# A row test of a DFT matrix, cut into pieces that alternate between two buffers, in an FNet and GLU kernel

## The chip, the core and the metric

The kernel runs on one core of a Trainium2 chip. The core has a matrix engine (TensorE, "PE" in the profile, its weight loads "PEld"), a vector engine (VectorE, DVE), an engine for activation functions (ScalarE, ACT), GpSimd (POOL) and SyncE (SP), which here issues nearly all DMAs. Each engine works through its own queue in order; semaphores tie the queues together. Sixteen DMA engines move the data. The metric is the device time of one execution in microseconds.

## The reference

Two kinds of layers are applied in turn, twice each, to x of 2048 rows and 640 columns. The first is a Fourier layer, given as dense matrices; the second a gated linear unit. The matrices and weights are inputs:

```python
def _A_ref(x, dft_seq_re, dft_seq_im, dft_hid_re, dft_hid_im):
    a = jnp.einsum("bsd,ed->bse", x, dft_hid_re)
    b = jnp.einsum("bsd,ed->bse", x, dft_hid_im)
    y = jnp.einsum("ts,bse->bte", dft_seq_re, a) - jnp.einsum("ts,bse->bte", dft_seq_im, b)
    return y

def _B_ref(x, w_gate, w_up, w_down):
    g = jnp.einsum("bsd,df->bsf", x, w_gate)
    u = jnp.einsum("bsd,df->bsf", x, w_up)
    h = _sigmoid(g) * u
    return jnp.einsum("bsf,fd->bsd", h, w_down)

x = x + _A_ref(_layernorm(x, axis=-1), A_dft_seq_re, A_dft_seq_im, A_dft_hid_re, A_dft_hid_im)
x = x + _B_ref(_layernorm(x, axis=-1), B_w_gate, B_w_up, B_w_down)
...
```

The inner width of the gated unit is 1728. After the two lines shown, both are applied once more.

## The kernel before

**Tiling.** The rows of x live in SBUF for the whole run, 16 tiles of 128 rows. One wide buffer (`big`) holds everything else: it is counted in units of 128 float32 columns, a planner (`Slots`) hands out ranges of units, and behind the planner's range lie two fixed buffers of 8 units, the *rooms* 0 and 1 (`room(k)`, with k taken modulo 2). All products are made of float16 parts: a matrix is split into a high part (on ACT, L236) and a low part (on DVE, L238), and three of the four cross products are summed in PSUM.

**Stages.** Each of the two layers has a Fourier stage and a gated stage. The Fourier stage folds rows and columns that a DFT matrix repeats with equal or opposite sign, so that a quarter of the work is left. Its results come back in four *quads* of row tiles: `combine` (L910), `join_hidden` (L917) and `add_hidden` (L930) add each quad's results to the rows of x, all on DVE. The gated stage goes over four blocks of 512 rows. In each block, gate and up products run over 14 column tiles j of the weights (13 of 128 and a tail), and then the down product (L1232) runs over four row tiles in two halves each. Block 0 uses `gate_up` (L1039), one step for each j. Blocks 1 to 3 use `seven` (L1085 with PSUM copies L1089 on ACT), one for each two j, a form with seven products in place of eight; it reads weights that `load_s` fetches with three DMAs (L1010, L1012, L1013: 320, 512 and 192 KB), and a transposed x that `pair_transpose` (L504) makes with DMA transposes before the block begins.

**Tests.** The folded way is right only if the DFT matrices have the symmetries of a DFT. So the kernel also reads the matrices whole and tests them: differences (or sums) of entries that should cancel are squared and summed on ACT (`square_sum`, L1264, one new column of `dsum` for each), and largest values are taken on DVE. At the end `test_all` compares the sums with a tolerance and sets a flag; if it is set, a plain version (`general`) runs after all. The matrix `ct` over rows is tested in both layers, in 42 pieces each, through the two rooms. The matrix `wh` over columns (real and imaginary, 640 by 640) is tested in the second layer alone, from the third down stage to the end of the last block's gate and up stage. `load_hidden(j)` loads 64 rows of both parts into room 0 and the 64 mirrored rows, in reverse order, into room 1 (L1339, two DMAs of 320 KB). `test_hidden(j)` takes the largest value (L1342), subtracts or adds the mirrored rows for each part (L1345) and the mirrored columns (L1346), and puts three squares on a list; `square_rest` makes them. Five such tests, each over both rooms, and one of row 0 cover the matrix.

**Order.** The instructions of every engine are laid out by a hand-made plan. The products are a list of *steps*; `at(u, f, ...)` puts other work at a place u in steps, and before each step (or within a `seven`, which spans two, in four places) the work due by then is issued to the queues. `block[b]` is the step at which the gate and up stage of block b begins; a block is 22 steps, 14 for gate and up and 8 for down. So a load at `block[2] + 15.5` is issued within the down stage of block 2. A queue is not reordered afterwards: an instruction that waits holds up all that stand behind it on its engine. SP's DMAs use eight semaphores in turn, so that a DMA is also behind the one issued eight before it.

Of the kernel before, what the change touches and what calls it, by code (L numbers as in the profile page):

```python
# [30 lines left out]
EC = EH + 1  # L31
# [147 lines left out]
@with_exitstack  # L179
def kernel(ctx: ExitStack, tc: tile.TileContext, x, ct, wh, wg, wu, wc, wd, out):  # L180
    nc = tc.nc
    pool = ctx.enter_context(tc.tile_pool(name="sb", bufs=1))
    psum = ctx.enter_context(tc.tile_pool(name="ps", bufs=1, space=bass.MemoryType.PSUM))
    dram = ctx.enter_context(tc.tile_pool(name="dr", bufs=1, space=bass.MemoryType.DRAM))

    big = pool.tile([P, (UNITS + 2 * CK) * UNIT], F32, name="big")
    acc = [psum.tile([P, 512], F32, name=f"acc{i}") for i in range(6)]
    flag = pool.tile([P, 1], I32, name="flag")
    with tc.manual_schedule():
        folded(ctx, tc, pool, dram, big, acc, flag, x, ct, wh, wg, wu, wc, wd, out)  # L190
    bad = nc.values_load(flag[0:1, 0:1], min_val=0, max_val=1,
                         skip_runtime_bounds_check_because="it is the result of a comparison")
    with tc.If(bad != 0):
        with tc.manual_schedule():
            general(tc, big, [acc[2 * i : 2 * i + 2] for i in range(4)], x, ct, wh, wg, wu, wc, wd, out)


def folded(ctx, tc, pool, dram, big, acc, flag, x, ct, wh, wg, wu, wc, wd, out):
    nc = tc.nc
# [60 lines left out]
    def at(u, f, *a):  # L260
        jobs[max(0, int(u // 1))].append((u, f, a))
# [993 lines left out]
    def new_sum():  # L1255
        n_sum[0] += 1
        return dsum[:, n_sum[0] - 1 : n_sum[0]]

    def new_max():
        n_max[0] += 1  # L1260
        return cmax[:, n_max[0] - 1 : n_max[0]]

    def square_sum(v, p=0):
        nc.scalar.activation(v, v, AF.Square, accum_out=new_sum()[p : p + v.shape[0]])  # L1264

    rest = []

    def square_rest():
        square_sum(*rest.pop(0))

    def room(k, n=CK):
        u = UNITS + CK * (k % 2)
        return big[:, u * UNIT : (u + n) * UNIT]
# [8 lines left out]
    def test_rows(r, k):  # L1282
        v = room(k)
        a, b, c, d = (v[:, 2 * P * g : 2 * P * (g + 1)] for g in range(4))
        same, other = (OP.subtract, OP.add) if r == 0 else (OP.add, OP.subtract)
        nc.vector.tensor_tensor(b, a, b, op=same)  # L1286
        nc.vector.tensor_tensor(d, c, d, op=same)
        for odd in range(2):
            nc.vector.tensor_tensor(c[:, odd::2], a[:, odd::2], c[:, odd::2], op=other if odd else same)  # L1289
        rest.append((v[:, 2 * P :], 0))  # L1290

    def load_cols(r, i, k):

# [5 lines left out]
    def test_cols(r, i, k):  # L1299
        v = room(k)[: P if i < NB else 1]  # L1300
        a, d, c, b = (v[:, 256 * g : 256 * (g + 1)] for g in range(4))
        same, other = (OP.subtract, OP.add) if r == 0 else (OP.add, OP.subtract)
        nc.vector.tensor_reduce(new_max()[: a.shape[0]], a, axis=AX.X, op=OP.max, apply_absolute_value=True)
        nc.vector.tensor_tensor(b, b, a[:, ::-1], op=same)
        nc.vector.tensor_tensor(d, d, c[:, ::-1], op=same)
        nc.vector.tensor_tensor(c, c, a[:, ::-1], op=other if i in (2, 3) else same)
        rest.append((v[:, 256:], 0))

    def load_edges(r):

# [7 lines left out]
    def test_edges(r):  # L1318
        v = held["ce", r].f32
        nc.vector.tensor_reduce(new_max(), v[:, :40], axis=AX.X, op=OP.max, apply_absolute_value=True)  # L1320
        nc.vector.tensor_reduce(new_max()[0:1], v[0:1, 40:42], axis=AX.X, op=OP.max, apply_absolute_value=True)
        if r == 0:
            for a, b in ((0, 16), (32, 36)):
                for odd in range(2):
                    d = v[:, b + odd : 2 * b - a : 2]
                    nc.vector.tensor_tensor(d, v[:, a + odd : b : 2], d, op=OP.add if odd else OP.subtract)
            nc.vector.tensor_tensor(v[0:1, 41:42], v[0:1, 40:41], v[0:1, 41:42], op=OP.subtract)
            square_sum(v[:, 16:32])
            square_sum(v[:, 36:40])
            square_sum(v[0:1, 41:42])  # L1330
        else:
            square_sum(v[:, :40])
            square_sum(v[0:1, 40:42])
        drop("ce", r)

    def load_hidden(j):

        for k, (row, step) in enumerate(((1 + 64 * j, D), (D - 1 - 64 * j, -D))):
            nc.sync.dma_start(room(k)[:, :D], bass.AP(wh.tensor, row * D, [[D * D, 2], [step, 64], [1, D]]))  # L1339

    def test_hidden(j):
        nc.vector.tensor_reduce(new_max(), room(0)[:, :D], axis=AX.X, op=OP.max, apply_absolute_value=True)  # L1342
        for r, op in enumerate((OP.subtract, OP.add)):
            a, b = (room(k)[64 * r : 64 * r + 64, :D] for k in range(2))
            nc.vector.tensor_tensor(b, a, b, op=op)  # L1345
            nc.vector.tensor_tensor(a[:, 1:EH], a[:, 1:EH], a[:, D - 1 : EH : -1], op=op)  # L1346
            rest.append((a[:, :EC] if r else a[:, 1:EH], 64 * r))
        rest.append((room(1)[:, :D], 0))

    def load_hidden_first():  # L1350

        for r in range(2):
            nc.sync.dma_start(room(r)[0:1, :D], wh[r, 0:1, :])

    def test_hidden_first():
        a, b = (room(r)[0:1, :D] for r in range(2))
        nc.vector.tensor_reduce(new_max()[0:1], a, axis=AX.X, op=OP.max, apply_absolute_value=True)
        nc.vector.tensor_tensor(a[:, 1:EH], a[:, 1:EH], a[:, D - 1 : EH : -1], op=OP.subtract)
        rest.append((a[:, 1:EH], 0))
        rest.append((b, 0))  # L1360

    def test_all():

# [95 lines left out]
    for layer in range(2):  # L1459
# [10 lines left out]
        block = []  # L1470
# [23 lines left out]
        if first:  # L1494
            for b in range(NB):
# [12 lines left out]
                else:  # L1508
                    for k in range(2):
                        v = d0 + 4 * k  # L1510
# [37 lines left out]
        for q in range(1, NB):  # L1548
            for n, (f, *a) in enumerate(((combine, 0), (combine, 1), (join_hidden, 0), (add_hidden, 0), (join_hidden, 1),
                                         (add_hidden, 1))):  # L1550
                at(block[0] + 1.6 + (0.8 * n if q == 1 else 6 * q - 7 + n), f, q, *a)
        for b in range(1, NB):
            for i in range(2):
                u = block[b] - 8 + 1.2 * i
# [35 lines left out]
        if first:  # L1590
            for j in range(NF):
                if 3 <= j < NF:
                    u = block[0] + j - 1.5
                else:
                    u = block[1] - 8 + 1.5 * j
# [21 lines left out]
        at(u0, test_edges, layer)  # L1617
        if not first:
            tests = [(load_hidden, test_hidden, (j,), 3) for j in range(EH // 64)]
            tests.append((load_hidden_first, test_hidden_first, (), 2))  # L1620
            for q, (load, test, key, n) in enumerate(tests):
                u = block[2] + 15.5 + 3 * q
                at(u, load, *key)
                at(u + 2, test, *key)
                for k in range(n):
                    at(u + 2.2 + 0.25 * k, square_rest)
            at(block[3] + 16, test_all)

    for u, step in enumerate(steps):
        if step is None:  # L1630
# [4 lines left out]
                      key=lambda j: j[0])  # L1635
# [163 lines left out]
```

## Time and profile before

| What | us |
|---|---|
| three runs | 1215.63, 1217.84 (median), 1218.98 |
| the profiled execution, its own time | 1217.2 |
| its span in the profile | 1215.3 |
| first product of the first layer's block 0 (gate and up) to the last block's end in that layer | 96.89 to 625 |
| second layer's last gate and up stage | 1046.44 to 1164.25 |
| its down stage | 1164.25 to 1208.8 |

| Engine | busy us | share of the span |
|---|---|---|
| PE | 1144.1 | 94% |
| PEld | 864.6 | 71% |
| DVE | 737.7 | 61% |
| ACT | 500.7 | 41% |
| POOL | 169.1 | 14% |

How to read it: times are from the start of the span. A row of the timeline has its start, its length, engine, line, operation, what is written and read, how many, and in brackets how long the engine had been idle before it and what ended that. "big" is the wide buffer, "acc" a PSUM bank, "in_wh" the matrix over columns in HBM, "kept_w" and "kept_s" the split weights that the kernel wrote to HBM in the first layer. PEclk is the share of TensorE's clock that was granted. In the DMA rows the first is the busy share of the 16 engines in tenths and the second the rate, each in 40 equal slices of the stretch asked for. A share of a queue is the time of its packets over the time of 16 engines.

### The profile page before, as it was taken

To read this page: it belongs to the slowest core of one execution; us is meant where nothing else is said; L and a number is where in the kernel's file an instruction comes from. 1 tells how busy PE (TensorE), PEld (TensorE's weight loads), DVE (VectorE), ACT (ScalarE), POOL (GpSimd) and SP (SyncE) were. 2 spreads that over 40 slices of the span, in tenths; PEclk is the share of its full clock that TensorE was granted. 3 is DMA by queue.
4 is the path that set the end of the run, shared out by engine and by line. 5 is a ranking of instruction groups with operands and counts; after the bars stand their busy time and mean duration, and the time that the engine had idled before them with its cause. 6 is when DMAs were issued, how large, how long until landed. Compare 5 with 4: busy or idle time off the path is not lost.

```text
span 1215.3 us, 22619 instructions
## 1 busy us (share of the span) xinstructions
PE 1144.1 (94%) x8784; PEld 864.6 (71%) x8784; DVE 737.7 (61%) x1590; ACT 500.7 (41%) x1066; POOL 169.1 (14%) x361
## 2 busy tenths in 40 slices
PE   5699989999999999999999999999999999578997
PEld 2367435788878887888766645788878887457875
DVE  7694899657747675766335768556854675224430
ACT  5665444255525552565115214145533552034410
POOL 3423555210002010100011001000100010000000
PEclk9799999999999999999999999999999999879899
DMA  9352887868596959688025425879498847545301
GB/s 276 112 161 88 278 292 265 209 228 214 154 223 189 265 179 227 209 226 232 1 66 177 143 67 162 222 207 279 134 244 245 265 148 83 148 137 150 113 13 36
DMA packets 219711, 214.75 MB, mean 177 GB/s; under 512 B 67886, under 2 KB 175303, under 8 KB 219594
## 3 DMA queue, kind: packets, MB, share of 16 engines
q1 hardware_dynamic: 218954, 210.59, 59.7%
q0 software_dynamic: 640, 2.62, 0.6%
q8 instruction: 71, 1.16, 0.4%
q14 instruction: 46, 0.38, 0.1%
HBM read 169.39 MB, written 30.40 MB: 164 GB/s over the span
## 4 chain that ended last, share of the span: by engine, by line
PE 76%; DVE 6%; DMA 6%; issue 4%; ACT 3%; SPq 2%; POOL 2%; ACTq 0%; POOLq 0%; DVEq 0%
PE acc L1085 34%; PE acc L1232 25%; PE acc L1039 11%; DMA big<-in_wh 4%; PE acc L1168 2%; PE acc L845 2%; PE acc L763 2%; DVE big L238 1%; SPq L504 1%; DMA big<-kept_w 1%; ACT big L236 1%; DVE big L1064 0%; DVE big L498 0%; DVE big L1345 0%; POOL quad L397 0%
## 5 line engine op out<-in xcount | busy, mean ns | idle before, releaser
L1085 PE MATMUL acc<-big 128*128 128x256 f16 x4212 | 471.1, 275 | 28.7 <-ACT big L1089 23.4
L1085 PEld LDWEIGHTS <-big 128*128 128x128 f16 x4212 | 415.7, 99 | 81.5 <-issue 24.0
L1232 PE MATMUL acc<-big 128*128 128x320 f16 x2624 | 357.9, 299 | 0.6 <-DVE big L1219 0.6
L1232 PEld LDWEIGHTS <-big 128*128 128x128 f16 x2624 | 256.7, 98 | 100.5 <-ACT big L1218 0.9
L1089 ACT ACTIVATE big<-acc 128x256 f32<-128x256 f32 x312 | 117.1, 383 | 201.3 <-PE acc L1085 197.8
L1039 PE MATMUL acc<-big 128*128 128x512 f16 (+1 forms) x990 | 179.0, 342 | 8.0 <-DVE big L238 5.2
L1039 PEld LDWEIGHTS <-big 128*128 128x128 f16 x990 | 96.5, 98 | 89.7 <-DVE big L238 8.2
L1264 ACT ACTIVATE big<-big 128x768 f32<-128x768 f32 (+8 forms) x106 | 80.9, 763 | 164.1 <-DVE big L1289 95.0
L1153 DVE TENSOR_TENSOR big<-big 128x512 f16<-128x512 f32 x78 | 53.8, 690 | 123.4 <-ACT big L1152 123.4
L1247 DVE SCALAR_TENSOR_TENSOR big<-acc,big 128x320 f32<-128x320 f32 x64 | 28.3, 485 | 75.4 <-PE acc L1232 75.3
L1131 ACT ACTIVATE big<-big 128x512 f32<-128x512 f32 x78 | 47.8, 629 | 33.7 <-DVE big L1122 33.3
L238 DVE SCALAR_TENSOR_TENSOR big<-big 128x640 f16<-128x640 f32 (+6 forms) x81 | 59.1, 769 | 3.3 <-ACT big L236 3.2
L1286 DVE TENSOR_TENSOR big<-big 128x256 f32<-128x256 f32 x64 | 26.7, 417 | 52.6 <-DMA big<-in_ct 52.3
L1141 DVE SCALAR_TENSOR_TENSOR big<-acc,big 128x256 f32<-128x256 f32 x78 | 32.7, 419 | 39.4 <-PE acc L1085 32.8
L236 ACT ACTIVATE big<-big 128x640 f16<-128x640 f32 (+6 forms) x81 | 49.9, 668 | 15.6 <-DMA big<-big 4.6
L763 PE MATMUL acc<-big 128*128 128x256 f16 (+5 forms) x288 | 42.9, 309 | 12.4 <-ACT big L649 10.0
L1122 DVE TENSOR_TENSOR big<-big,acc 128x512 f32<-128x512 f32 x78 | 53.2, 682 | 2.2 <-PE acc L1085 2.0
L1152 ACT ACTIVATE big<-big 128x512 f16<-128x512 f32 x78 | 48.9, 627 | 7.1 <-DVE big L1143 5.8
L763 PEld LDWEIGHTS <-big 128*128 128x128 f16 (+1 forms) x288 | 31.1, 114 | 25.0 <-ACT big L649 12.9
L845 PE MATMUL acc<-big 128*128 128x321 f16 (+3 forms) x324 | 48.7, 301 | 0.2 <-ACT big L892 0.2
L845 PEld LDWEIGHTS <-big 128*128 128x128 f16 (+3 forms) x324 | 28.6, 96 | 19.3 <-issue 7.8
L1053 ACT ACTIVATE big<-acc 128x512 f32<-128x512 f32 x26 | 15.5, 596 | 64.1 <-DVE big L1064 34.4
(166 smaller groups left out, 990.0 us busy)
## 6 DMA issues: line engine op xcount, KB each, us to landing
big<-kept_w SPq DMA_DIRECT2D x125, 320.0 KB
big<-kept_s SPq DMA_DIRECT2D x75, 512.0 KB
big<-in_ct SPq DMA_DIRECT2D x256, 128.0 KB
big<-kept_w SPq DMA_DIRECT2D x78, 192.0 KB
kept_w<-big SPq DMA_DIRECT2D x41, 320.0 KB
big<-in_ct SPq DMA_DIRECT2D x32, 256.0 KB
kept_s<-big SPq DMA_DIRECT2D x13, 512.0 KB
big<-in_wg SPq DMA_DIRECT2D x16, 320.0 KB
```

The lines of the kernel that those rows point to most:

```text
L236: nc.scalar.activation(dh, src, AF.Copy, scale=s)
L238: nc.vector.scalar_tensor_tensor(dl, src, s, dh, op0=OP.mult, op1=OP.subtract)
L763: nc.tensor.matmul(o, xv[:, 384 * xp + c0 : 384 * xp + c0 + n], moving(r, cps[cp]), start=(i % 2 == 0 and r == 0 and xp == HI and cp == HI ...
L845: nc.tensor.matmul(ps[:m, :EC], z[:, at : at + m], w[:, 384 * wp : 384 * wp + EC], start=(d == 0 and zp == HI and wp == HI), stop=(d == ND ...
L1039: nc.tensor.matmul(ps, w[wp][:, d * P : (d + 1) * P], xt[:, xp, :], start=(d == 0 and wp == HI and xp == HI), stop=(d == ND - 1 and wp == LO))
L1085: nc.tensor.matmul(ps, wt, xt, start=start and n == 0, stop=n == len(todo) - 1, skip_group_check=not start)
L1089: nc.scalar.activation(dst, ps, AF.Copy)
L1122: nc.vector.tensor_tensor(v, v, other, op=OP.add)
L1152: nc.scalar.activation(s.parts[HI], v, AF.Copy)
L1153: nc.vector.tensor_tensor(s.parts[LO], v, s.parts[HI], op=OP.subtract)
L1232: nc.tensor.matmul(held["pd", e][0][:, :EH], held["ht", j].parts[hp][:, i * P : (i + 1) * P], held["w", 2, j].parts[wp][:, e * EH : (e + 1 ...
L1264: nc.scalar.activation(v, v, AF.Square, accum_out=new_sum()[p : p + v.shape[0]])
```

## The change

The test of `wh` is cut in another way. Symmetry over rows and symmetry over columns are now tested apart, each with its own reading of the matrix. For rows (`load_hidden_rows`, `test_hidden_rows`), each part is tested in four pieces of 80 rows and their 80 mirrored rows, eight pieces in all. A piece fits in one room: the 640 columns are five blocks of 128, a block's 80 rows stand on 20 partitions, four rows on each, so that 100 partitions are used, the rows in one half of the room and the mirrored ones in the other. Pieces alternate between the rooms. A piece needs two DMAs, one DVE operation over 512 columns and one square. For columns (`load_hidden_cols`, `test_hidden_cols`), each part's 321 first rows are read in three pieces of 128, 128 and 65 rows by 640 columns, each in one room, with a largest value, one subtraction or addition and one square each (one more square for a part of row 0). Loads, tests and squares have new places: a row piece every 1.7 steps with its test 2.8 steps after the load and its square 0.42 steps later, then a column piece every 0.9 steps with its test 1.4 steps after.

`square_sum` no longer takes a first partition; that renames lines only. And the additions of the quads in block 0 are laid out anew, in both layers: the third quad's six operations one step earlier, the last quad's six two steps later, so that all six of the last quad come after the gate and up stage, within the first down steps.

```diff
-    def square_sum(v, p=0):
-        nc.scalar.activation(v, v, AF.Square, accum_out=new_sum()[p : p + v.shape[0]])
+    def square_sum(v):
+        p = v.shape[0]
+        nc.scalar.activation(v, v, AF.Square, accum_out=new_sum()[:p])
...
-    def load_hidden(j):
-
-        for k, (row, step) in enumerate(((1 + 64 * j, D), (D - 1 - 64 * j, -D))):
-            nc.sync.dma_start(room(k)[:, :D], bass.AP(wh.tensor, row * D, [[D * D, 2], [step, 64], [1, D]]))
-
-    def test_hidden(j):
-        nc.vector.tensor_reduce(new_max(), room(0)[:, :D], axis=AX.X, op=OP.max, apply_absolute_value=True)
-        for r, op in enumerate((OP.subtract, OP.add)):
-            a, b = (room(k)[64 * r : 64 * r + 64, :D] for k in range(2))
-            nc.vector.tensor_tensor(b, a, b, op=op)
-            nc.vector.tensor_tensor(a[:, 1:EH], a[:, 1:EH], a[:, D - 1 : EH : -1], op=op)
-            rest.append((a[:, :EC] if r else a[:, 1:EH], 64 * r))
-        rest.append((room(1)[:, :D], 0))
...
+    def load_hidden_rows(r, k):
+
+        v = room(k)[: 20 * ND].rearrange("p (g n c) -> p g n c", g=2, c=P)
+        for g, (row, d) in enumerate(((1 + 80 * k, 1), (D - 1 - 80 * k, -1))):
+            nc.sync.dma_start(v[:, g], bass.AP(wh.tensor, (r * D + row) * D, [[P, ND], [d * D, 80], [1, P]]))
+
+    def test_hidden_rows(r, k):
+        a, b = (room(k)[: 20 * ND, 4 * P * g : 4 * P * (g + 1)] for g in range(2))
+        nc.vector.tensor_tensor(b, a, b, op=OP.subtract if r == 0 else OP.add)
+        rest.append(b)
+
+    def load_hidden_cols(r, j):
+        n = P if j < 2 else EC - 2 * P
+        nc.sync.dma_start(room(3 * r + j)[:n, :D], wh[r, j * P : j * P + n, :])
+
+    def test_hidden_cols(r, j):
+        a = room(3 * r + j)[: P if j < 2 else EC - 2 * P, :D]
+        nc.vector.tensor_reduce(new_max()[: a.shape[0]], a, axis=AX.X, op=OP.max, apply_absolute_value=True)
+        nc.vector.tensor_tensor(a[:, 1:EH], a[:, 1:EH], a[:, D - 1 : EH : -1], op=OP.subtract if r == 0 else OP.add)
+        rest.append(a[:, 1:EH] if r == 0 else a[:, :EC])
+        if r == 1 and j == 0:
+            square_sum(a[0:1, EC:])
...
-                at(block[0] + 1.6 + (0.8 * n if q == 1 else 6 * q - 7 + n), f, q, *a)
+                at(block[0] + 1.6 + (0.8 * n if q == 1 else 4 + n if q == 2 else 13 + n), f, q, *a)
...
-            tests = [(load_hidden, test_hidden, (j,), 3) for j in range(EH // 64)]
-            tests.append((load_hidden_first, test_hidden_first, (), 2))
-            for q, (load, test, key, n) in enumerate(tests):
-                u = block[2] + 15.5 + 3 * q
-                at(u, load, *key)
-                at(u + 2, test, *key)
-                for k in range(n):
-                    at(u + 2.2 + 0.25 * k, square_rest)
+            tests = [(load_hidden_rows, test_hidden_rows, (r, k), 15.5 + 1.7 * (4 * r + k), 2.8) for r in range(2)
+                     for k in range(4)]
+            tests += [(load_hidden_cols, test_hidden_cols, (r, j), 29.8 + 0.9 * (3 * r + j), 1.4) for r in range(2)
+                      for j in range(3)]
+            for load, test, key, u, later in tests:
+                at(block[2] + u, load, *key)
+                at(block[2] + u + later, test, *key)
+                at(block[2] + u + 1.15 * later, square_rest)
```

More of the change, by code (lines that the diff above doesn't have):

```diff
@@ L1261, in new_max @@
         return cmax[:, n_max[0] - 1 : n_max[0]]
-    def square_sum(v, p=0):
-        nc.scalar.activation(v, v, AF.Square, accum_out=new_sum()[p : p + v.shape[0]])
+    def square_sum(v):
+        p = v.shape[0]
+        nc.scalar.activation(v, v, AF.Square, accum_out=new_sum()[:p])
     rest = []
     def square_rest():
-        square_sum(*rest.pop(0))
+        square_sum(rest.pop(0))
     def room(k, n=CK):
@@ L1289, in test_rows @@
             nc.vector.tensor_tensor(c[:, odd::2], a[:, odd::2], c[:, odd::2], op=other if odd else same)
-        rest.append((v[:, 2 * P :], 0))
+        rest.append(v[:, 2 * P :])
     def load_cols(r, i, k):
@@ L1306, in test_cols @@
         nc.vector.tensor_tensor(c, c, a[:, ::-1], op=other if i in (2, 3) else same)
-        rest.append((v[:, 256:], 0))
+        rest.append(v[:, 256:])
     def load_edges(r):
@@ L1334, in test_edges @@
         drop("ce", r)
-    def load_hidden(j):
-        for k, (row, step) in enumerate(((1 + 64 * j, D), (D - 1 - 64 * j, -D))):
-            nc.sync.dma_start(room(k)[:, :D], bass.AP(wh.tensor, row * D, [[D * D, 2], [step, 64], [1, D]]))
-    def test_hidden(j):
-        nc.vector.tensor_reduce(new_max(), room(0)[:, :D], axis=AX.X, op=OP.max, apply_absolute_value=True)
-        for r, op in enumerate((OP.subtract, OP.add)):
-            a, b = (room(k)[64 * r : 64 * r + 64, :D] for k in range(2))
-            nc.vector.tensor_tensor(b, a, b, op=op)
-            nc.vector.tensor_tensor(a[:, 1:EH], a[:, 1:EH], a[:, D - 1 : EH : -1], op=op)
-            rest.append((a[:, :EC] if r else a[:, 1:EH], 64 * r))
-        rest.append((room(1)[:, :D], 0))
[L1350 to L1360, printed above, removed]
+    def load_hidden_rows(r, k):
[16 more added lines that the diff above has]
+            square_sum(a[0:1, EC:])
     def test_all():
```

## The prediction

> **What bounds the kernel now.** I read the page's chain first, then the busy time of the four undisturbed gate-and-up stages beside the last one (each is some 740 matmuls of one row block), then the chain in order of time inside the last one, and last the DMA rates there. The chain's shares:
>
> ```profile
> PE 76%; DVE 6%; DMA 6%; issue 4%; ACT 3%; SPq 2%; POOL 2%; ACTq 0%; POOLq 0%; DVEq 0%
> PE acc L1085 34%; PE acc L1232 25%; PE acc L1039 11%; DMA big<-in_wh 4%; PE acc L1168 2%; PE acc L845 2%; PE acc L763 2%; DVE big L238 1%; SPq L504 1%; DMA big<-kept_w 1%; ACT big L236 1%; DVE big L1064 0%; DVE big L498 0%; DVE big L1345 0%; POOL quad L397 0%
> ```
>
> TensorE sets the end, except for 4% of `in_wh` transfers, which only the row test of the hidden matrix reads at that time. Busy time by stage:
>
> ```profile
> core 0: us, PE busy (x) PEld busy (x) DVE busy (x) ACT busy (x) POOL busy (x), PEclk, DMA share, GB/s
> 365.65:446.21 80.56, 80.56 (x740) 72.18 (x739) 58.36 (x147) 45.79 (x107) 12.80 (x36) 1.00 0.74 212
> ...
> 796.37:876.93 80.56, 80.56 (x740) 72.18 (x739) 56.73 (x137) 44.14 (x101) 5.49 (x17) 1.00 0.73 214
> 921.49:1001.89 80.40, 80.40 (x739) 72.05 (x738) 49.22 (x123) 43.62 (x101) 5.43 (x16) 1.00 0.66 210
> 1046.44:1164.25 117.81, 89.13 (x742) 75.93 (x740) 44.11 (x85) 42.13 (x105) 0.00 (x0) 0.87 0.35 111
> ```
>
> The same work takes 80.5 us three times, at a granted clock of 1.00, and 117.8 us in the last block of the second layer: 28.7 us idle, and 89.1 - 80.5 = 8.6 us more busy at a clock of 0.87. The excess is 37.3 us. TensorE's own rows and the chain there:
>
> ```profile
> 1046.44 3.44 PE L1085 MATMUL acc<-big 128*128 128x256 f16 x30
> 1065.61 13.20 PE L1085 MATMUL acc<-big 128*128 128x256 f16 x99 [15.73 <-ACT big L1089]
> 1085.09 20.24 PE L1085 MATMUL acc<-big 128*128 128x256 f16 x159 [6.28 <-ACT big L1089]
> ```
>
> ```profile
> 1024.44 10.45 SPq L504
> ...
> 1042.92 18.13 DMA big<-in_wh
> 1061.07 0.83 DVE big L1345
> ...
> 1065.31 15.93 DMA big<-in_wh
> ...
> 1087.43 15.54 DMA big<-in_wh
> ...
> 1113.76 13.40 DMA big<-kept_w
> ```
>
> Read it backwards: the PSUM copies L1089 stand on ACT behind the test's squares L1264, these wait for the subtractions L1345 on DVE, and these for a load. A test fills both rooms, so its successor's load waits for its squares: load, test, squares, load run in series, 16 to 18 us each, and on SP the weight loads (L1010 to L1013) stand behind the waiting load; the last 13.4 us are such weights. Why a load takes so long:
>
> ```profile
> GB/s 340 394 404 436 430 368 332 399 335 74 57 46 57 51 63 46 46 57 46 57 46 57 51 51 51 51 57 46 57 46 57 51 51 51 51 51 51 57 34 6
> ```
>
> These are 40 slices of 1043 to 1061 us: weights move at some 400 GB/s, then `in_wh` alone at 51 GB/s, an eighth, as of 2 engines in 16. One 328 KB load is 128 packets of 2,560 bytes: 6.4 us, 64 packets of 100 ns on each engine, and a pair 12.8 us. The source pattern's outermost count is 2 (real and imaginary).
>
> **The new loads.** A piece is two DMAs of 400 packets of 512 bytes, outermost count 5 in the source and 100 partitions in the room. No such load is in the trace. Nearest rows are the ct loads (L1280: 512-byte packets, outermost count 16), alone in 699.2 to 701.6 us:
>
> ```profile
> DMA packets 1121, 0.58 MB, mean 243 GB/s; under 512 B 77, under 2 KB 1097, under 8 KB 1121
> ...
> q1 hardware_dynamic: 1121, 0.58, 82.6%
> ```
>
> 0.826 x 16 engines x 2.4 us / 1,121 = 28.3 ns a packet. The trace's two patterns ran on as many engines as the outermost count; I take five for five. Then a DMA is 80 packets, 2.26 us, and a piece 4.5 us. Bounds: 16 engines 1.4 us, two engines 11.3 us, one 22.6 us; and with 100 ns a packet on five, 16 us.
>
> The Trainium skill, "DMA: Bandwidth & Descriptors", section "Why a DMA increments its semaphore by 16 and not by 1", says that a DMA runs on the largest number up to 16 that divides the slowest counts of both its patterns. That gives 2 for the old load (2 and 128; the 51 GB/s agree) and 5 for the new one (5 and 100), so 4.5 us; no run here shows a five yet.
>
> **Can SP's queue deliver?** From the first load (1018.79) to the weights of step 8 of the block, SP issues all eight pieces (8x), the second pair of transposes (5.8 us, the first pair's row), six weight triples of 1.05 MB (2.5 us each at 410 GB/s, 15) and two stores (1.6): 22.4 + 8x, and some 2 to land. Unstalled, step 8 starts at 1046.44 + 8/14 x 80.5 = 1092.4. So 8x may be 1092.4 - 1018.8 - 24.4 = 49.2, x = 6.15 us (38 ns a packet). At 4.5 us (36 in all) 13 us are to spare, and the pieces are scheduled 1.7 steps of 5.75 = 9.8 us apart.
>
> **Who waits.** A test stands 2.8 steps (16 us) behind its load instead of two. Pieces alternate between rooms, so one loads while the other is tested. On DVE the evictions L1247 and then L1121/L1122 stand behind a test, on ACT L1089 behind a square, on SP the weight triples behind a load that waits for its room's square. The earliest critical one is the third piece: its square stands on ACT behind the block's first two L1089 and ahead of those that TensorE needs from 1049.9 (1046.44 + 3.44) on. The first load needs 4.5 us where it needed 12.8, so the transposes that waited 10.45 us leave by about 1030; one piece (4.5) and two triples (5) follow, and the third piece lands near 1045. After its test and square (0.7 us each) the cover is some 3.5 us, the least of all; without it each late us is a us of TensorE. The column pieces are 128 rows of 2,560 bytes, outermost count 128 like the weights: 8 packets an engine, 0.8 us, hidden.
>
> Engine work hardly changes. DVE loses 5 x (0.82 + 2 x 0.82 + 2 x 0.48) + 1.3 = 18.4 us and gets eight subtractions at 0.69 (L1153, 512 wide) and six of 0.82 + 0.48: 13.3 us; ACT gets about 10 for 10. Both are busy under 60 of 80 us in the other blocks, whose ct tests cost TensorE nothing. **This term: -37.3 us** (37.2 to 37.4 by the three stages), the clock's 8.6 included, since no idle stretch is left.
>
> **The moved additions.** In the second layer nothing waits: TensorE is busy all of 660 to 752 us. In the first, 147 to 207 us, DVE bounds the stage (55.7 busy of 60):
>
> ```profile
> 175.82 8.34 PE L1039 MATMUL acc<-big 128*128 128x512 f16 x30 [2.06 <-DVE big L238]
> ...
> 206.41 34.12 PE L1232 MATMUL acc<-big 128*128 128x320 f16 x250 [0.57 <-DVE big L1219]
> ```
>
> The third quad's six operations each go one step earlier, so up to one more (L930, 1.55 us) lies ahead of the splits L238 that TensorE waits for; the last quad's two combines (L910, 0.89 each) leave the stage, but only the 0.57 us at its end can return. Moved under the first down, they lie beside 44 us of L1232; the ops there delay L1247 by under 2 us, and banks are next needed 7 us after its last one (233.2 to 240.4). Their units stay taken longer: a gate load issued at 145.91 comes to wait for L991, which ended at 146.41. From -0.6 to +2.0; **I take +0.5**.
>
> **Sum:** span 1215.3 - 37.3 + 0.5 = 1178.5; the profiled run took 1217.2, 1.9 more, and the median is 0.6 above that: **1181.0 us**, own range 1179 to 1184.
>
> **Rivals.**
> - *A wait remains* (the third piece late, or packets dearer on five engines that also carry their share of all else). For it: cover of 3.5 us; 13 us of slack end at 38 ns. Against: 28.3 ns was measured with all 16 engines loaded. At 50 ns x = 8, 8x - 49.2 = 14.8 us lost: 1196.
> - *Too few engines*, the other side: the loads run on two engines or one, because the trace only shows 2 and 16. At two, 90.4 - 49.2 = 41 us are lost against 37 gained: 1222; at one, 181 - 49 = 132: 1313. It turns slower from x = 10.8 us.
> - *It does not do what it says*: the eight tests are as serial as the five were, because load k+2 still waits for square k on an ACT queue behind L1089, and SP holds the weights behind it. The gain is then given back: about 1217. Against it: squares need only 0.8 us, and the wait is now for TensorE's own progress.
>
> **Chances.** Forecast 0.77, remaining wait 0.14, too few engines 0.05, no effect 0.04. Faster by over 0.3% (3.7 us, about what this measurement can tell from none) 0.91, same 0.04, slower 0.05. The range: 1177 (the moved additions gain, runs spread) to 1196 (a remaining wait at 50 ns); what lies above is about 0.14.
>
> **What will show it.** Right: the last block's gate-up stage takes 80 to 82 us at a clock of 1.00; no L1085 waits for L1089 or kept_w; `in_wh` moves at 80 to 90 GB/s (five engines) in stretches under 5 us; the second transposes leave before 1031. Wrong: 51 GB/s or less in the new loads; L1345 waiting for `in_wh` with L1247 or L1121 behind it past 1050; stage 96 to 207 us longer by over 2 us.

## The result, and the profile after

| What | before | after |
|---|---|---|
| four runs, median (us) | 1217.59 | 1184.35 |
| lowest to highest | 1215.63 to 1218.98 | 1182.33 to 1186.93 |
| profiled execution, own time | 1217.2 | 1182.33 |
| its span | 1215.3 | 1180.5 |
| last gate-up stage | 117.81 | 80.65 |
| mean granted clock | 0.977 | 0.985 |

The ratio is 0.9729, with a 95% interval from 0.9706 to 0.9753: faster by 33 us. The forecast was 1181.0. The stage's 117.81 us run to the end of its last product; from its first product to the first of the down stage, as the 80.65 after and all stages below are taken, it was 117.65 before, so it is 37.0 us shorter. Line numbers are now those of the changed kernel: the row loads are L1341, their subtraction L1345, the column loads L1350, their tests L1354 and L1355, the squares L1265, the edge load of `ct` L1314.

The chain of waits of the changed kernel, by engine and by line:

```profile
PE 84%; DMA 5%; issue 3%; DVE 3%; ACT 2%; POOL 2%; SPq 1%; POOLq 0%; ACTq 0%; DVEq 0%
PE acc L1085 38%; PE acc L1232 30%; PE acc L1039 10%; PE acc L1168 2%; PE acc L845 2%; PE acc L763 2%; DVE big L238 1%; DMA kept_o<-big 1%; DMA big<-in_wu 1%; ACT big L236 1%; DMA kept_c<-big 1%; DMA big<-in_x 1%; DMA big<-in_wh 0%; DMA big<-kept_w 0%; DMA big<-in_wd 0%
```

`in_wh` had 4% of the chain and now rounds to 0; TensorE's share went from 76 to 84%. Busy time by stage, the last three gate-up stages of the second layer:

```profile
797.17:877.73 80.56, 80.56 (x740) 72.17 (x739) 56.39 (x137) 43.76 (x101) 5.36 (x16) 1.00 0.74 214
922.29:1002.85 80.56, 80.56 (x740) 72.18 (x739) 49.05 (x122) 42.64 (x99) 4.83 (x16) 1.00 0.62 196
1047.41:1128.06 80.65, 80.65 (x740) 72.17 (x739) 39.06 (x79) 39.40 (x101) 0.00 (x0) 1.00 0.54 172
```

The last one is now as long as its neighbours, busy throughout and at a clock of 1.00. TensorE's own rows there have no bracket, so no wait:

```profile
1002.69 44.72 PE L1232 MATMUL acc<-big 128*128 128x320 f16 x328
1047.24 71.56 PE L1085 MATMUL acc<-big 128*128 128x256 f16 x654
1118.64 1.80 PE L1168 MATMUL acc<-big 128*128 128x256 f16 x15
```

The third and the fourth piece of the row test are issued one behind the other. This is how they move once the weights ahead of them have landed and they are nearly alone on the DMA engines (first row the busy share in tenths, second the rate, 40 slices of 1043 to 1049 us):

```profile
DMA  6643333333333333333333333333333333333333
GB/s 224 207 149 94 102 104 109 109 106 113 109 106 113 106 106 109 109 106 113 106 109 109 106 113 109 106 109 109 102 113 109 106 113 106 109 109 106 113 109 102
```

They move at 108.5 GB/s with three tenths of the engines busy: five engines in 16, 21.7 GB/s each, which is 23.6 ns for a packet of 512 bytes. A piece of 409.6 KB takes 3.8 us.

The span fell by 34.8 us and the stage by 37.0. The 2.2 us between are, against the profile before: the products begin 2.0 us sooner, the stretch from the first layer's block 0 to its block 1 is 0.5 longer, the road from there to the last gate-up stage 2.2 longer, and what follows the stage 1.4 longer. (That stretch is counted, here and in the tables below, from the run of 300 products L1039 that stands behind the transposes to the first product of block 1: 101.28 to 240.37 us before, 99.30 to 238.92 after.) Of the 2.2 on the road, 1.4 lie between the layers (624.7 to 671.4 us), where the profile before had a clock of 1.00 and this one 0.96. It is lost on 31 products that stand behind waits of the same length in both profiles, first before, then after:

```profile
638.37 3.56 PE L763 MATMUL acc<-big 128*128 128x256 f16 x31 [0.47 <-DVE big L654]
```

```profile
637.80 4.96 PE L763 MATMUL acc<-big 128*128 128x256 f16 x31 [0.47 <-DVE big L654]
```

Another 0.7 is a wait that the kernel before did not have, and it turned out to be the more interesting part:

```profile
297.44 13.93 PE L1085 MATMUL acc<-big 128*128 128x256 f16 x126 [0.72 <-DMA big<-kept_w]
```

### The profile page after: what moved, and what is told of

Its sections match the earlier page's. It is cut to its first block, busy times and chain, and to the rows that moved or that the text cites. A ratio compares the mean times of both kernels' runs of the same rounds, so it can differ in the third digit from the quotient of the medians.

```text
span 1180.5 us, 22636 instructions
## 1 busy us (share of the span) xinstructions
PE 1136.0 (96%) x8784; PEld 861.3 (73%) x8784; DVE 738.1 (63%) x1583; ACT 497.5 (42%) x1062; POOL 168.6 (14%) x361
## 4 chain that ended last, share of the span: by engine, by line
PE 84%; DMA 5%; issue 3%; DVE 3%; ACT 2%; POOL 2%; SPq 1%; POOLq 0%; ACTq 0%; DVEq 0%
PE acc L1085 38%; PE acc L1232 30%; PE acc L1039 10%; PE acc L1168 2%; PE acc L845 2%; PE acc L763 2%; DVE big L238 1%; DMA kept_o<-big 1%; DMA big<-in_wu 1%; ACT big L236 1%; DMA kept_c<-big 1%; DMA big<-in_x 1%; DMA big<-in_wh 0%; DMA big<-kept_w 0%; DMA big<-in_wd 0%
## 5 line engine op out<-in xcount | busy, mean ns | idle before, releaser
L1085 PE MATMUL acc<-big 128*128 128x256 f16 x4212 | 462.9, 273 | 0.7 <-DMA big<-kept_w 0.7
L1089 ACT ACTIVATE big<-acc 128x256 f32<-128x256 f32 x312 | 116.4, 381 | 211.6 <-PE acc L1085 209.7
L1039 PE MATMUL acc<-big 128*128 128x512 f16 (+1 forms) x990 | 179.6, 344 | 8.7 <-DVE big L238 4.9
L1039 PEld LDWEIGHTS <-big 128*128 128x128 f16 x990 | 96.9, 98 | 90.6 <-DVE big L238 7.2
L1265 ACT ACTIVATE big<-big 128x768 f32<-128x768 f32 (+8 forms) x104 | 79.4, 764 | 128.0 <-DVE big L1290 93.3
L1287 DVE TENSOR_TENSOR big<-big 128x256 f32<-128x256 f32 x64 | 26.7, 417 | 56.9 <-DMA big<-in_ct 56.6
L1141 DVE SCALAR_TENSOR_TENSOR big<-acc,big 128x256 f32<-128x256 f32 x78 | 32.7, 419 | 38.4 <-PE acc L1085 31.4
L497 ACT ACTIVATE big<-big 128x384 f16<-128x384 f32 (+2 forms) x48 | 28.9, 647 | 32.0 <-DVE big L479 28.9
```

The source lines that it names most:

```text
L1039: nc.tensor.matmul(ps, w[wp][:, d * P : (d + 1) * P], xt[:, xp, :], start=(d == 0 and wp == HI and xp == HI), stop=(d == ND - 1 and wp == LO))
L1085: nc.tensor.matmul(ps, wt, xt, start=start and n == 0, stop=n == len(todo) - 1, skip_group_check=not start)
L1089: nc.scalar.activation(dst, ps, AF.Copy)
L1265: nc.scalar.activation(v, v, AF.Square, accum_out=new_sum()[:p])
```

## The experiments

Ten kernels ran. Each time stands beside runs of the kernel before on the same chip, and the ratios are to those.

### The two halves of the change, each alone

`e1_rows_only` is the changed kernel with the old layout of the additions:

```diff
-                at(block[0] + 1.6 + (0.8 * n if q == 1 else 4 + n if q == 2 else 13 + n), f, q, *a)
+                at(block[0] + 1.6 + (0.8 * n if q == 1 else 6 * q - 7 + n), f, q, *a)
```

> The changed kernel with the row additions of the quads laid out as before, so the new test alone. Theory (the whole gain is the last gate-up stage): that stage takes 80.5 to 81 us without a gap, as in the changed kernel (80.65), and the time is 1184.35 less the 0.5 us that the moved additions cost in the profiles (first product of the first layer's block 0 to that of block 1: 139.62 us with them moved, 139.09 before): 1183.9, ratio to the kernel before 0.972 to 0.973, with 139.1 us in that stretch. Rival (the moved additions carry a share of the gain): 1186 or more, ratio above 0.974. Second rival (they cost more than the profile of one run shows): under 1182, ratio under 0.971.

`e2_adds_only` is the kernel before with the same line turned the other way.

> The kernel before with the moved additions alone, the old test kept. Theory: 1217.6 + 0.5 = 1218.1, ratio 1.0004, no change that the times can tell; the last gate-up stage stays at 117 to 119 us; the stretch from the first layer's block 0 to its block 1 is 139.6 us and the 0.57 us wait of L1232 on L1219 is gone. Rival (the additions pay): under 1215, ratio under 0.998. Second rival (they cost): above 1220, ratio above 1.002.

| Kernel | median us | ratio, 95% interval | last gate-up stage | block 0 to block 1, first layer |
|---|---|---|---|---|
| e1_rows_only (5 runs) | 1182.67 | 0.9714, 0.9699 to 0.9730 | 80.65 | 138.80 |
| e2_adds_only (12 runs) | 1221.44 | 1.0028, 1.0014 to 1.0043 | 118.63 | 139.92 |

The row test alone makes the whole gain. The moved additions alone cost 3.4 us (1.7 to 5.2 by the interval), where 0.5 was expected; it is the second rival of that expectation that came. Only 0.8 us of it is in the stretch that they lie in (139.92 against 139.09 before). Where the rest is shows further down.

### Slower loads with the rooms still in turn

`e3_slow_32` cuts each row load in two, of three and of two column blocks:

```diff
-            nc.sync.dma_start(v[:, g], bass.AP(wh.tensor, (r * D + row) * D, [[P, ND], [d * D, 80], [1, P]]))
+            for n, m in ((0, 3), (3, 2)):
+                nc.sync.dma_start(
+                    v[20 * n : 20 * (n + m), g],
+                    bass.AP(wh.tensor, (r * D + row) * D + n * P, [[P, m], [d * D, 80], [1, P]]))
```

> The changed kernel with each row load cut into a DMA of three column blocks and one of two: the same packets into the same places, rooms and order as changed, only on three and two DMA engines, so that two engines have 160 packets of a half piece in place of 80. At the 23.6 ns a packet of the changed kernel's trace (409.6 KB at 108.5 GB/s on five engines) a piece takes 2 x 160 x 23.6 ns = 7.55 us. Theory (the prediction's sum of SP's queue): the loss is 8 x 7.55 - 49.2 = 11.2 us, so 1195.6, ratio 0.982; the last gate-up stage is some 92 us with waits of L1085 on L1089 or on kept_w. Rival (the alternation of the rooms alone hides the loads, whatever their speed): the stage stays at 80.7 us and the time at 1182 to 1187, ratio 0.973. Second rival (each piece late is a us of TensorE from the third piece on, since its cover is now seen to be about 1.5 us): three pieces 3.8 us later each less 1.5, about 10 us by the third piece alone and more behind it, 1194 to 1215.

`e4_slow_222` cuts it in three of two blocks each; 120 partitions are used and the fourth block is tested twice:

```diff
+            for q, n in enumerate((0, 2, 3)):
+                nc.sync.dma_start(
+                    v[40 * q : 40 * q + 40, g],
+                    bass.AP(wh.tensor, (r * D + row) * D + n * P, [[P, 2], [d * D, 80], [1, P]]))
```

> As the run before, with three DMAs of two column blocks each (the fourth block is read and tested twice, since five is odd), all on two DMA engines: 240 packets on each, 2 x 240 x 23.6 ns = 11.3 us a piece. Theory (the queue's sum): 8 x 11.33 - 49.2 = 41.4 us lost, more than the 37.2 that were won: 1225.8, ratio 1.007, slower than the kernel before although rooms alternate. Rival (alternation hides the loads): 1182 to 1187, ratio 0.973. Between them: a loss that grows by less than 8 us for each us of x says that not all eight pieces stand ahead of the weights that set the end: half of the sum would be 1205, ratio 0.990.

| Kernel | median us | ratio, 95% interval | last stage | idle in it | SP at the row loads |
|---|---|---|---|---|---|
| e3_slow_32 | 1206.14 | 0.9910, 0.9894 to 0.9925 | 102.95 | 18.3 | 59.55 |
| e4_slow_222 | 1235.90 | 1.0161, 1.0142 to 1.0180 | 132.13 | 42.4 | 88.07 |

The last column is the sum of SP's rows for the eight pieces, with the small gaps inside them. The rival "alternation hides the loads, whatever their speed" is out: with the rooms in turn and packets of the same size on two engines (a fifth more of them) the kernel is slower than before. The rate in e4 between 1060 and 1075 us, 44 GB/s in nearly every slice, is two engines at the same 23 ns a packet:

```profile
GB/s 59 44 44 44 42 44 44 44 44 42 44 44 42 44 44 44 44 44 42 44 42 44 44 44 44 44 42 44 44 44 42 44 44 44 42 44 44 44 44 44
```

The Trainium skill, "DMA: Bandwidth & Descriptors", section "Why a DMA increments its semaphore by 16 and not by 1", gives two engines for these loads and five for the changed kernel's, and both traces agree.

28.5 us more on SP's queue made the stage 29.2 us longer, so the slope of the prediction's sum holds. Its constant does not: both stages lost 10 to 11 us more than the sum said. The time of e3 also lies in the range of its second rival (1194 to 1215), in which the third piece comes late, and that wait is there, 7.16 of the 18.3 us. TensorE's rows of e3 show where they go:

```profile
1048.15 6.06 PE L1085 MATMUL acc<-big 128*128 128x256 f16 x54
1061.37 18.23 PE L1085 MATMUL acc<-big 128*128 128x256 f16 x150 [7.16 <-ACT big L1089]
1088.83 13.59 PE L1085 MATMUL acc<-big 128*128 128x256 f16 x108 [9.23 <-DMA big<-kept_w]
1102.57 11.96 PE L1085 MATMUL acc<-big 128*128 128x256 f16 x108 [0.15 <-DVE big L1122]
1116.29 25.72 PE L1085 MATMUL acc<-big 128*128 128x256 f16 x234 [1.76 <-DMA big<-kept_w]
```

First the third piece's square holds up the PSUM copies, then the weights behind the loads are late, and the last restart is at 1116.29. In the changed kernel, where nothing waits, the same product stands 45.8 us behind the first of the stage; in e3, whose stage begins at 1048.15, that would be 1094.0. From the first row load (1020.52) to the weights of that product SP's queue in e3 holds 59.55 us of row loads, the transposes (6.50), two stores (3.42), seven weight triples (18.75), 1.3 of gaps, and 6.3 until the last one has landed. The prediction counted six triples at 2.5 us, 1.6 us for the two stores and 2 us to land. So 36.2 us are taken by other work and not 24.4, and 37.3 us are free for row loads, not 49.2; 59.55 - 37.3 = 22.3 is what the stage lost. An estimate from these numbers: the changed kernel's eight pieces of 3.8 us, 30 us in all, leave 7 us to spare, not 13. It may be more, since its issues of row loads lasted only 18.6 us on SP.

### Fast loads with the rooms in series

`e5_one_room` puts all pieces into room 0. With one room a test has to come before the next load, so the tests also stand nearer to their loads:

```diff
-        v = room(k)[: 20 * ND].rearrange("p (g n c) -> p g n c", g=2, c=P)
+        v = room(0)[: 20 * ND].rearrange("p (g n c) -> p g n c", g=2, c=P)
...
-            tests = [(load_hidden_rows, test_hidden_rows, (r, k), 15.5 + 1.7 * (4 * r + k), 2.8) for r in range(2)
+            tests = [(load_hidden_rows, test_hidden_rows, (r, k), 15.5 + 1.7 * (4 * r + k), 1.4) for r in range(2)
...
-            tests += [(load_hidden_cols, test_hidden_cols, (r, j), 29.8 + 0.9 * (3 * r + j), 1.4) for r in range(2)
+            tests += [(load_hidden_cols, test_hidden_cols, (r, j), 29.8 + 0.9 * (3 * r + j), 0.7) for r in range(2)
```

> The changed kernel with every piece in room 0, so load, test, square and the next load run in series as in the kernel before; the test stands 1.4 steps behind its load (columns 0.7) and the square 0.21 (0.1) behind that, so that a square comes before the next load. Theory (it is the speed of a load that counts, not the alternation): a piece on five engines is 3.8 us, its test and square 1.5 us, and a load is placed every 9.8 us, so the series fits in the spacing: stage 80.5 to 83 us, time 1182 to 1187, ratio 0.971 to 0.975. Rival (the series of load, test and square through one place is what cost the 37 us, alternation is what won them): with eight pieces in place of five in the same stage, each waiting for ACT's queue, the stage stays above 95 us and the time above 1198, ratio above 0.984.

`e6_old_fwd16` is the kernel before with its forward rows loaded by one DMA for each part:

```diff
-            nc.sync.dma_start(room(k)[:, :D], bass.AP(wh.tensor, row * D, [[D * D, 2], [step, 64], [1, D]]))
+            if k == 1:
+                nc.sync.dma_start(room(k)[:, :D], bass.AP(wh.tensor, row * D, [[D * D, 2], [step, 64], [1, D]]))
+            for r in range(2 * (1 - k)):
+                nc.sync.dma_start(room(k)[64 * r : 64 * r + 64, :D], bass.AP(wh.tensor, (r * D + row) * D, [[step, 64], [1, D]]))
```

> The kernel before with one edit: the 64 forward rows of a test are read by two DMAs, one for each part, whose outermost count is 64 and not 2; the mirrored rows keep their DMA with an outermost count of 2. So a pair takes 6.4 us (one DMA on two engines) where it took 12.8, both rooms still in series and the additions as before. Theory (speed of the load): the series of 16 to 18 us a test becomes 10 to 12, under the 17 us between two tests, and five tests hold SP's queue for 5 x 6.4 = 32 us, inside the some 37 us that the two slowed kernels show to be free (59.6 us of loads on SP's queue cost 22.3 us of stage, 88.1 us cost some 51): the stage is 80.5 to 83 us and the time 1180 to 1185, ratio 0.970 to 0.973. Rival (both rooms in series is the cause): half of the excess at most comes back, stage above 95 us, time above 1198, ratio above 0.984. Third: a load whose outermost count is 64 does not run on more engines than two: no change, 1218.

| Kernel | median us | ratio, 95% interval | last stage | idle in it |
|---|---|---|---|---|
| e5_one_room | 1194.12 | 0.9803, 0.9782 to 0.9825 | 86.53 | 4.2 |
| e6_old_fwd16 | 1194.88 | 0.9796, 0.9775 to 0.9816 | 93.32 | 10.1 |

Both expectations failed, from both sides: speed alone does not bring the whole gain, and series alone does not keep half of the loss. In e5 the stage is 5.9 us longer than in the changed kernel. Nearly all of it comes from one place, a wait of 3.93 us and some 1.5 us more for the products behind it, at a clock of 0.86 from 1059 to 1070 us:

```profile
1049.11 6.06 PE L1085 MATMUL acc<-big 128*128 128x256 f16 x54
1059.10 67.10 PE L1085 MATMUL acc<-big 128*128 128x256 f16 x600 [3.93 <-ACT big L1089]
```

ACT's rows of e5 name the piece; the two rows L1265 are the squares of the third and the fourth:

```profile
1050.69 0.63 ACT L1265 ACTIVATE big<-big 100x512 f32<-100x512 f32 x1 [9.24 <-DVE big L1345]
...
1051.32 0.64 ACT L1089 ACTIVATE big<-acc 128x256 f32<-128x256 f32 x2
1058.05 0.63 ACT L1265 ACTIVATE big<-big 100x512 f32<-100x512 f32 x1 [6.10 <-DVE big L1345]
...
1058.68 1.18 ACT L1089 ACTIVATE big<-acc 128x256 f32<-128x256 f32 x4
```

The copies L1089 stand behind the next square, which waits, through the subtraction L1345, for a load that could not start before the square ahead of it. In the changed kernel the same rows are close, but hold:

```profile
1048.75 0.38 ACT L1089 ACTIVATE big<-acc 128x256 f32<-128x256 f32 x1 [0.27 <-PE acc L1085]
1049.10 0.63 ACT L1265 ACTIVATE big<-big 100x512 f32<-100x512 f32 x1
1049.64 0.19 ACT L1265 ACTIVATION_READ_ACCUMULATOR big<-big 100x1 f32 x1
1051.37 0.38 ACT L1089 ACTIVATE big<-acc 128x256 f32<-128x256 f32 x1 [1.55 <-PE acc L1085]
```

The third piece's square ends at 1049.8 and the next copy is wanted at 1051.4: 1.55 us of cover. The piece itself had been issued at 1037.8, but the loads ran alone only from 1043.4 on, since two weight triples, and a store of 0.3 MB that GpSimd issues, were ahead of it on the DMA engines; its test could start at 1048.37.

So, by stage: 117.7 us (two engines, series), 93.3 (half the load time, series), 86.5 (five engines, series), 80.7 (five engines, in turn), and 132.1 for two engines in turn with eight pieces. The speed of the loads is most of the gain. The alternation, with the later tests that it allows, is worth 5.9 us at that speed; by the medians of e5 and of the changed kernel on the same chip (1188.35, below) it is 5.8.

### What the moved additions cost, and why

`e7_after_again` is the changed kernel unedited, in more rounds.

> The changed kernel itself, unedited, in more rounds, to set it against the run with the old layout of the additions (1182.67 us, ratio 0.9714, 0.9699 to 0.9730). Theory (the moved additions cost 1.5 us or more here as they did alone, 1.0028): 1184 to 1186.5, ratio 0.9725 to 0.9745. Rival (they cost 0.5 us at most): 1182.5 to 1183.5, ratio 0.9712 to 0.9720.

`e8_third_quad` has only the third quad's move:

```diff
-                at(block[0] + 1.6 + (0.8 * n if q == 1 else 4 + n if q == 2 else 13 + n), f, q, *a)
+                at(block[0] + 1.6 + (0.8 * n if q == 1 else 4 + n if q == 2 else 11 + n), f, q, *a)
```

> The changed kernel with only the third quad's six operations one step earlier and the last quad's where they were before. Theory (what costs is work put ahead of the splits L238 that TensorE waits for, so the third quad's move): the stretch from the first layer's block 0 to block 1 is 139.5 us or more and the time 1184 to 1187, ratio 0.9725 or more. Rival (what costs is the last quad beside the down products, whose units stay taken longer): stretch 138.8 us and 1182 to 1183.5 as with the old layout, ratio 0.971 to 0.972.

The changed kernel took 1188.35 us this time (0.9747, 0.9730 to 0.9763), on another chip than e1, and the third quad alone 1191.97 (0.9776, 0.9751 to 0.9801); both are above the times that the theories gave. Both have 139.90 us from block 0 to block 1, so the theory on that stretch holds: the third quad's work, one step earlier, stands ahead of splits that TensorE waits for. But that is 1 us. e8 has two waits more besides, 1.42 us at 242 and 1.23 at 430. The rest is in block 1 of the first layer, which the change does not touch. TensorE and SP in e7:

```profile
301.71 15.59 PE L1085 MATMUL acc<-big 128*128 128x256 f16 x126 [2.96 <-DMA big<-kept_w]
```

```profile
252.10 0.53 SPq L1013 DMA_DIRECT2D big<-kept_w  x1
272.28 0.82 SPq L1314 DMA_DIRECT2D big<-in_ct  x2
```

```profile
SPq L1314 <- DVE big L1141: 19.9, 1, 19.9
```

and SP in e1, the same new test with the old layout:

```profile
249.99 0.53 SPq L1013 DMA_DIRECT2D big<-kept_w  x1
251.35 0.84 SPq L1314 DMA_DIRECT2D big<-in_ct  x2
```

SP stands 19.9 us at one small load, until L1141 of block 1 is done at 272 us. The likely reason is that the planner, with units of the additions taken at other times, gives the load a unit that L1141 still uses. All seven profiles so far with the third quad moved have this stand of 19.9 to 20.6 us, and the four with the old layout (before, e1, e6, e10) do not. All weights behind it are late, and near 300 us TensorE waits for them: 0.72 us in the changed kernel's first profile, 1.26 in e2, 1.61 in e3, 1.07 in e4, 1.56 in e5, 2.96 in e7, 3.12 in e8, and not at all with the old layout. After the two waits near 3 us the granted clock was lower too: those 126 products took 15.59 us in e7 and 15.27 in e8, against 13.93 in the other five.

`e9_edges_room` takes that one wait away, by loading the edges into the idle room and keeping the unit taken, so that no other place moves:

```diff
-        v = take(1, "ce", r, high=True).f32
+        v = (take(1, "ce", r, high=True), room(1)[:, :P])[1]
...
-        v = held["ce", r].f32
+        v = room(1)[:, :P]
```

> The changed kernel with one edit: the edge test of ct (load_edges, L1314) loads into the idle room 1 and no longer into the planner's unit; the unit stays taken, so that every other place and order is as changed. In all four profiles with the moved additions SP stands 19.9 to 20.6 us at this load in the first layer, for a unit that L1141 gives back (with the old layout it does not), and L1085 then waits 0.7 to 3.1 us for kept_w near 300 us. Theory (this wait is what the moved additions cost, beyond the 0.8 us of their stretch): L1314 leaves near 252 us, no wait of L1085 for kept_w near 300 us, and the time falls from the changed kernel's 1188.35 (ratio 0.9747) to 1183.5 to 1186, ratio 0.971 to 0.973. Rival (SP's wait is idle time of a queue that has time, and the weights are late by contention): the wait of L1085 stays and the ratio is 0.974 to 0.976.

`e10_rows_again` is e1's kernel on the same chip as e9.

> The new test with the additions laid out as before, once more, on the same chip as the run above. Theory: ratio 0.971 to 0.973 again (0.9714 the first time), with the stretch from block 0 to block 1 at 138.8 us and no wait of L1085 near 300 us; equal to the run above or up to 1 us under it, and under the changed kernel itself (0.9729 and 0.9747) by 2 to 4 us. Rival (the two runs of the changed kernel and the one of this differ only by chips): 0.9735 to 0.975.

| Kernel | median us | ratio, 95% interval | block 0 to block 1 | wait near 300 us |
|---|---|---|---|---|
| e7_after_again (on another chip than the other two) | 1188.35 | 0.9747, 0.9730 to 0.9763 | 139.90 | 2.96 |
| e9_edges_room | 1183.69 | 0.9708, 0.9691 to 0.9724 | 139.92 | none |
| e10_rows_again | 1181.83 | 0.9691, 0.9674 to 0.9707 | 138.75 | none |

SP and TensorE in e9:

```profile
252.75 0.53 SPq L1013 DMA_DIRECT2D big<-kept_w  x1
253.33 1.06 SPq L1314 DMA_DIRECT2D big<-in_ct  x2
```

```profile
241.60 71.56 PE L1085 MATMUL acc<-big 128*128 128x256 f16 x654
```

The load leaves at 253, the 654 products run without a wait, and the ratio falls by 0.0039, some 4.7 us: 2.96 of wait and 1.66 of clock are 4.6. Between e9 and e10, on one chip, remain 1.9 us, of which the stretch is 1.2; their five runs do not overlap (1183.40 to 1184.89, 1180.76 to 1182.58), so e10 was better than expected, which was at most 1 us under e9. The row test without the moved additions beats both kernels, and is the version to keep: by the intervals of e7 and e10, each against the kernel before on its own chip, it is faster than the changed kernel, while the first pair (0.9729 and 0.9714) could not tell them apart.

## Why the prediction was right, and where it was off

- **The last stage, -37.3 us: right.** It measured -37.0 (-37.2 by the 117.81 that the prediction took), clock included, and nothing waits in it.
- **Five engines: right; the packet price was high.** A piece took 3.8 us and not 4.5, at 108.5 GB/s and not 80 to 90. The 28.3 ns came from the share of time that packets took, and by that measure a new packet has 26.9 ns (1,063 packets with 35.8% of 16 engines from 1043.5 to 1048.5 us). That share is the whole time of 5.7 engines, so the records of packets overlap, and the 23.6 ns of the rate are what counts. The second transposes left at 1029.93, by 1030 as stated.
- **The queue's sum: right in form, without a reason, and wrong in its constant.** The slope is near 1 us for each us of SP's queue, and 37 us were free and not 49.2. The kernel turns slower from x = (37.3 + 37.0) / 8 = 9.3 us and not 10.8. The sum charges SP with the whole time of a transfer. The profile before did not show that: an issue of the old loads took SP 0.50 to 0.60 us for a transfer of 6.4. For loads of many small packets, one behind the other, it came out so (last section), which the prediction could not know: that part is luck.
- **The third piece as the tightest place: right; its cover was too large.** Landing near 1045 was predicted and 1048.3 measured; the cover is 1.55 us and not 3.5. The term left out is the time in which the piece shares the DMA engines with the weights ahead of it. e5 shows what comes when it is gone.
- **The moved additions, +0.5 (-0.6 to +2.0): the step that failed.** They cost 3.4 us alone, 1.8 by the first pair of ratios (0.9729 and 0.9714) and 6.8 by those of e7 and e10. The stretch was as stated (+0.5 to +1.2). The prediction saw that "their units stay taken longer" and looked for it at a gate load in the same stage; it struck a load 100 us later. The forecast without this term, 1180.5, is 1.3 to 2.2 us under the times of the row test alone. How near 1181.0 came is in part luck: it was 3.35 us low against the first four runs and 7.35 against e7's, of the same kernel.
- **The rival "too few engines": its case did not come, and its price was low.** 1222 was given for two engines; e4 ran on two, with the 11.3 us a piece that the rival took, and measured 1235.9, for the constant of the queue again.
- **The rival "does not do what it says": wrong as a whole, right in part.** Without the alternation the stage is 5.9 us longer, at the very queue that it named (squares on ACT ahead of L1089).

Still open: the 1.4 us at the end, why 31 products between the layers run at a lower clock in one profile than in another, and why the wait near 300 us is 0.7 us in one run of the changed kernel and 3.0 in another. No run has the last quad's later place without the third quad's move, so what it costs by itself is not shown.

## What to carry to other kernels

Look at the slowest dimension of a DMA's patterns before anything around it: the same loads at five engines, and with a fifth more bytes at two, made 51 us of difference here (80.7 and 132.1), more than any order of the work hid. Add up everything that stands in the issuing queue between a load and the first thing that starves, with its landing time; what is left is the budget for the loads, and beyond it each us counted in full here. When work is moved in a kernel whose memory a planner hands out, compare the waits of the issuing queue over the whole run, not in the stage that was edited.

## What the hardware showed that was not expected

A DMA's time on SP depends on what stands ahead of it on its engines. These are the issues of all row loads in the changed kernel and in e3 (shortest, median and longest in ns):

```profile
L1341 SPq DMA_DIRECT2D big<-in_wh x16: 742/810/3737, 1019.6 to 1078.5; - x16
```

```profile
L1342 SPq DMA_DIRECT2D big<-in_wh x32: 668/1812/4216, 1020.5 to 1105.2; - x32
```

A row load of 400 packets took 0.81 us of SP where the engines were free; in e3 and e4 loads of 80 packets an engine, one behind the other, took 1.81 us each, which is 22.6 ns a packet, the engines' own speed. The Trainium skill, "Perfetto Trace Analysis", section "DMA Instruction — HWDGE (DVE, Sync)", says that an issue lasts until all descriptors are generated and that engines begin early when the buffer is full; the two durations fit that. Waits for a semaphore are not in these durations: they stand as gaps, and of the 59.55 us in e3 the 32 issues are 56.9. So loads of many packets blocked the queue itself, not only their readers. The old loads, slower but with 64 packets an engine, took 0.50 to 0.60 us of issue each; what held the queue there were waits of a load for the transfer and the squares of the test before it.

The granted clock fell after the wait of 2.96 us of TensorE in e7 (0.91 over 299 to 318 us) and not after 1.61 in e3 (13.93 us for the same 126 products); with the 1.66 us of slower products the wait in e7 cost half as much again. But the length of a wait does not settle it. In block 0 of the kernel before, 30 products behind a wait of 2.06 us took 8.34 us at a clock of 0.80; in e1 as many behind the same wait ran at 1.00. Between the layers the 31 products shown above, behind waits of 0.4, 0.5, 1.3 and 0.5 us, had a clock of 1.00 in one profile and 0.71 in the other.
